# Lightning attention with a shrunk-tanh MLP: another order for the first group, tied sums, and a last product in three banks

## The chip, the cores and the metric

The kernel runs on one NeuronCore of a Trainium2 chip. The metric is the device time of one execution in microseconds (us), given as the median of several runs. A core has TensorE (PE, matrix products; the loads of its weights are listed apart as PEld), VectorE (DVE), ScalarE (ACT), GpSimd (POOL) and SyncE (SP, which here only issues DMAs). Each engine works off its own queue in order. Products land in PSUM[...].

## The reference, cut to what matters

Sizes: B = 4 sequences, H = 8 heads, S = 768 positions, D = 64; 3072 tokens, d_model 512, d_ff 2048. All in fp32, though w_in and w_out arrive as float64.

```python
# attention, in blocks; state kv_state per (b, h)
intra = einsum('bhic,bhjc->bhij', qb, kb) * Dmask
intra = einsum('bhij,bhjd->bhid', intra, vb)
inter = einsum('bhid,bhde->bhie', qb * lam_pow, kv_state)
out   = intra + inter
kv_state = lam_block * kv_state + einsum('bhsd,bhse->bhde', kb * rev_pow, vb)
# MLP on x, the attention output with tokens as rows
h = x @ w_in
g = h - tanh(h)
y = g @ w_out
```

## The kernel before

The sequence is cut into 6 groups `g` of 128 positions; a group holds a chunk of 128 positions of each of the 4 sequences `b`, so 512 tokens. The attention of a group goes in two halves of two chunks, `bs = (0, 1)` and `(2, 3)`. Four functions do a half:

- `att_transpose` (L251): q and k come in natural layout (`q_nat`, `k_nat`, `v_nat`, each 256 KB) and are transposed on PE against the identity (L264); ACT copies them to SBUF (L265). From the second group on, VectorE also scales q with the powers `fwd` (L269). From the third group on q and k are loaded otherwise, and this needs no PE.
- `att_scores` (L272): the products of k and q (L279, tile `sp`), and on VectorE the multiplication with the decay mask (L283, tile `ss`).
- `att_state` (L286): VectorE scales k in place (L294), PE forms k-transposed times v of both chunks (L299, tile `kv`), and the state takes it up. In the first group it is a plain copy out of PSUM (L306, on VectorE).
- `att_out` (L308): PE forms the state's part (L324, not in the first group) and the scores times v (L330, tile `op`), and ACT copies the result to `xt` (L334).

The tile pool keeps 2 buffers for q, 3 for k and 4 for v, so the fourth k of the first group waits until the first chunk's k has been read for the last time, in its state products. All loads of q, k, v and w_in are issued on SP's queue, in `load` (L126) and `load_weights` (L173); those of w_out and of the factors, and nearly all stores, on POOL's.

The weights come as 64-bit words. `weights(n)` (L183) brings the count of processed blocks to `n`: each block of 512 KB is loaded to `raw` (4 buffers) and rounded to fp32 by `round_block` (L217): two ACT operations (L227, L229) and four VectorE operations (L230, L232, L234, L236). w_in has 16 blocks, four for each quarter `u` of d_ff; w_out has 16, two for each `kt`.

The first group runs plain products: `up_plain(u, c)` (L467: products L473, tanh L476, subtraction L478) for 4 quarters `u` and 4 parts `c`, and `down_plain(kt)` (L482: products L490) for 8 steps `kt`. Between the steps the attention of the second group is done, and `sums_out` (L206) forms the combinations of w_out, which are stored as `factors` in DRAM. `powers` (L100) fills `fwd`, `sums_in(u)` (L198: L201 to L204) forms the combinations of w_in that the other five groups need. Those groups run a Strassen-Winograd form with seven products instead of eight: `up` (L389, products L397) and `down` (L431, products L439), in the order 1, 2, 6, 5, 7, 4, 3. In `down` products 1, 6, 7 and 4 accumulate one on another in one bank, `y`, and 5 and 3 in another, `z`; product 2 has the bank `w`. `evict` (L366) copies or adds the banks to the output tiles `o`: after product 7 the fourth output (L379, L380), after product 3 the part `12` (L386), stored by the lines under `finish` (L452; L460 for the last one, which goes in two halves).

The order of instructions on each engine is not simply that of the code. A scheduler sets it when the program is built: it goes by program order as priority, but where an instruction is not ready by its own model of times, a later one that is ready is taken first. `tc.keep_in_program_order(ins)` ties an instruction behind everything that was traced before it on its engine. Before the change only the transposes and k scalings of later groups (L259, L296) are tied. The main order around the change reads:

```python
p0, p1 = attention(0)      # pieces: transpose, scores, out, state for (0,1) and (2,3)
run(p0)
run(p1[0:1]); weights(1); run(p1[1:2]); weights(2); run(p1[2:4])
weights(KI); powers()
```

The `sums_in(u)` are traced after the last `down_plain` step.

Of the kernel before, what the change touches and what calls it, by code (L numbers as in the profile page):

```python
# [14 lines left out]
AL = mybir.AluOpType  # L15
# [8 lines left out]
def kernel(  # L24
# [75 lines left out]
    def powers():  # L100
        for j in range(2):
            nc.vector.tensor_copy(fwd[ts(j, 64), :, 0], lam_all.rearrange("s (p j) -> s j p", j=2)[ts(j, 64), j, :])
        m = 1
        while m < BLK:
            nc.vector.tensor_tensor(fwd[:, :, m:2 * m], fwd[:, :, 0:m], fwd[:, :, m - 1:m].to_broadcast([128, NP, m]),
                                    op=AL.mult)
            m *= 2
# [11 lines left out]
    def load_natural(g, b, names):  # L119
        for name, src, bufs in (("q", q, 2), ("k", k, 3), ("v", v, 4)):  # L120
            if name in names:
                x = io.tile([128, H, D], F32, name=f"{name}_nat", tag=name, bufs=bufs)
                nc.sync.dma_start(out=x, in_=src[b, :, ts(g, BLK), :].rearrange("h s d -> s h d"))
                raw[g, b][name] = x
# [73 lines left out]
    def sums_in(u):  # L198
        a11, a12, a21, a22 = (w1[u][:, 2 * c:2 * c + 2, r] for r, c in ((0, 0), (0, 1), (1, 0), (1, 1)))
        s1, s2, s4 = (ws[u][:, x] for x in range(3))  # L200
        nc.vector.tensor_tensor(s1, a21, a22, op=AL.add)  # L201
        nc.vector.tensor_tensor(s2, s1, a11, op=AL.subtract)
        nc.vector.tensor_tensor(a21, a11, a21, op=AL.subtract)
        nc.vector.tensor_tensor(s4, a12, s2, op=AL.subtract)  # L204

# [80 lines left out]
    def att_state(g, bs):  # L286
# [18 lines left out]
        else:  # L305
            nc.vector.tensor_copy(st, kv)  # L306

# [58 lines left out]
    def evict(key, n, dst, finish):  # L366

        y, z, w = (banks.get((key, x)) for x in "yzw")
        halves = [slice(None)] if key != ("down", NG - 1) else [slice(0, 256), slice(256, 512)]
        if n == 1:  # L370
# [6 lines left out]
        elif n == 7:  # L377
            for x in halves:
                nc.scalar.activation(dst(22)[:, x], y[:, x], AF.Copy)  # L379
            nc.vector.tensor_tensor(dst(22), dst(22), z, op=AL.add)  # L380
            finish(22, dst(22))
        elif n == 4:
            finish(21, y)
        elif n == 3:
            for x in halves:
                nc.vector.tensor_tensor(dst(12)[:, x], dst(12)[:, x], z[:, x], op=AL.add)  # L386
            finish(12, dst(12))
# [43 lines left out]
    def down(g, n):  # L431
        load_factor(stream.index((g, n)) + 2)
        wb = blks.pop((g, n))
        t, first = product_bank(("down", g), n)
        c = HIDAT[FACT[n][0]]
        for m in range(2):
            for kt in range(KH):
                a = hid[g, kt // 2, c].rearrange("q (m c) -> q m c", m=2)[:, kt % 2, ts(m, 128)]
                nc.tensor.matmul(out=t[:, m, :], lhsT=a, rhs=wb[:, kt, :], start=first and m == 0 and kt == 0,  # L439
                                 stop=kt == KH - 1, skip_group_check=True)  # L440
# [11 lines left out]
        def finish(c, src):  # L452
# [4 lines left out]
            o = dst(c).rearrange("q (m c) -> q m c", m=2)  # L457
            if g == NG - 1 and c == 12:
                for m in range(2):
                    nc.sync.dma_start(out=rows[:, m], in_=o[:, m])  # L460
            else:
                nc.gpsimd.dma_start(out=rows, in_=o)

# [37 lines left out]

    p0, p1 = attention(0)
    run(p0)
    run(p1[0:1])
    weights(1)
    run(p1[1:2])
    weights(2)
    run(p1[2:4])
    weights(KI)
    powers()  # L510
    for u in range(NU):
        for c in (11, 21, 12, 22):
            up_plain(u, c)
            weights(ready["done"] + 1)
    p0, p1 = attention(1)
    weights(len(blocks) - 2 * (KH - 2))
    more = [p0[0:1], p0[1:2], p0[2:], p1[0:1], p1[1:2], p1[2:]]
    for kt in range(KH):
# [4 lines left out]
        if kt < len(more):  # L523
            run(more[kt])
    for u in range(NU):
        sums_in(u)
    stage_open.__exit__(None, None, None)
# [53 lines left out]
```

## Time and profile before

| What | Value |
|---|---|
| Runs | 700.61, 700.79, 699.34 us; median 700.61 |
| Profiled execution | 699.61 us, of which the span is 697.8 |
| PE busy | 681.0 us, 98% of the span |
| VectorE, ACT, POOL busy | 353.0, 167.0, 55.9 us |
| PE's first operation | 5.10 us |
| First record of `up_plain`, first of `down_plain` | 31.44 us, 88.26 us |
| First product of the second group after `down_plain` | 161.5 us |
| End of the last product | 694.1 us |
| HBM read, written | 75.50 MB, 13.63 MB |

The span is what the profile shows between the first and the last event on the core; the 1.8 us beyond it lie around the program. Times of single instructions are from this one execution. In the lists, `L123` is a line of the kernel, `out<-in` the tiles, `xN` a count, and a bracket holds the idle time of the engine before the instruction and what ended it. `PEclk` or "granted clock" is the share of full speed that TensorE was given.

### The profile page before, as it was taken

Reading aid. Unit: us, or ns where it says so; the run is one execution under the profiler, and the core shown is the slowest. Engines: PE = TensorE matmul, PEld = TensorE weight load, DVE = VectorE, ACT = ScalarE, POOL = GpSimd, SP = SyncE. Lnnn points to the kernel's source line nnn. Section 1 sums busy time; section 2 is a strip of 40 time slices with the busy share of each in tenths; the row PEclk is TensorE's granted clock in tenths of the full one; section 3 lists DMA queues with packets and bytes.
Section 4 is the critical chain, followed back from the end, with each engine's and each line's share of the span. In section 5 each row is a group of like instructions: output and inputs, shape, how many; then the busy total and the mean of one; then the engine's idle time right before and its main releaser. Section 6 shows DMA issues by size and latency. Waiting matters only on the chain.

```text
span 697.8 us, 10361 instructions
## 1 busy us (share of the span) xinstructions
PE 681.0 (98%) x4096; PEld 571.2 (82%) x4096; DVE 353.0 (51%) x608; ACT 167.0 (24%) x281; POOL 55.9 (8%) x96
## 2 busy tenths in 40 slices
PE   6799999999999999999999999999999999999997
PEld 5688845557888888888888888888888888888886
DVE  4697988671566341456532346813346712254501
ACT  2554523323331010331000332001232101233100
POOL 0000312211000001000111000001000101000100
PEclk9899999999999999999999999999999999999999
DMA  9789957847225666263555702455700332400343
GB/s 167 175 209 241 257 163 232 248 123 212 34 32 129 167 172 178 34 117 92 131 179 138 188 0 70 118 160 157 177 1 1 121 136 80 147 1 0 113 145 105
DMA packets 143999, 89.82 MB, mean 129 GB/s; under 512 B 129808, under 2 KB 130064, under 8 KB 139472
## 3 DMA queue, kind: packets, MB, share of 16 engines
q0 software_dynamic: 11232, 58.46, 24.6%
q1 hardware_dynamic: 132576, 30.71, 23.2%
q8 instruction: 32, 0.52, 0.3%
q14 instruction: 15, 0.12, 0.1%
q10 hardware_dynamic: 144, 0.00, 0.0%
HBM read 75.50 MB, written 13.63 MB: 128 GB/s over the span
## 4 chain that ended last, share of the span: by engine, by line
PE 87%; DMA 5%; DVE 4%; ACT 1%; issue 1%; SPq 1%; ACTq 0%; DVEq 0%; POOLq 0%
PE y L439 20%; PE y L397 20%; PE z L439 10%; PE z L397 10%; PE op L490 7%; PE w L439 5%; PE w L397 5%; PE op L330 3%; PE sp L279 3%; DMA raw<-in_moe_w_in_dram 2%; DMA raw<-in_moe_w_out_dram 2%; PE op L324 1%; PE kv L299 1%; DVE g L478 1%; DMA k_nat<-in_k_dram 1%
## 5 line engine op out<-in xcount | busy, mean ns | idle before, releaser
L439 PE MATMUL y<-wb,g 128*128 128x256 f32 x640 | 142.3, 380 | 0.7 <-ACT o L379 0.7
L439 PEld LDWEIGHTS y<-wb,g 128*128 128x128 f32 x640 | 120.9, 190 | 18.1 <-ACT o L379 1.1
L397 PE MATMUL y<-xt,w 128*128 128x256 f32 x320 | 73.6, 380 | 0.0
L407 ACT ACTIVATE th<-g 128x512 f32<-128x512 f32 x60 | 37.8, 630 | 140.3 <-DVE g L373 86.1
L397 PEld LDWEIGHTS y<-xt,w 128*128 128x128 f32 x320 | 60.5, 190 | 8.9 <-issue 0.6
L490 PE MATMUL op<-wt,g 128*128 128x512 f32 x128 | 57.0, 597 | 1.7 <-DVE g L478 1.7
L408 DVE TENSOR_TENSOR g<-g,th 128x512 f32<-128x512 f32 x60 | 41.4, 689 | 32.5 <-ACT th L407 32.5
L426 POOL DMA_DIRECT2D wb<-factors x35 | 19.0, 544 | 477.5 <-PE y L439 366.8
L473 PE MATMUL h<-xt,w 128*128 128x256 f32 x256 | 56.7, 382 | 0.3 <-DVE w L236 0.2
L473 PEld LDWEIGHTS h<-xt,w 128*128 128x128 f32 x256 | 48.6, 191 | 8.1 <-DVE w L236 1.5
L283 DVE TENSOR_TENSOR ss<-sp,mask 128x512 f32<-128x512 f32 x48 | 30.9, 682 | 47.8 <-PE sp L279 47.8
L490 PEld LDWEIGHTS op<-wt,g 128*128 128x128 f32 x128 | 23.7, 190 | 30.0 <-issue 26.1
L380 DVE TENSOR_TENSOR g<-g,z 128x512 f32<-128x512 f32 x20 | 13.7, 685 | 49.9 <-ACT g L379 49.9
L397 PE MATMUL w<-xt,w 128*128 128x256 f32 x160 | 37.8, 379 | 0.0
L397 PE MATMUL y<-tt,w 128*128 128x256 f32 x160 | 37.8, 379 | 0.0
L397 PE MATMUL z<-tt,ws 128*128 128x256 f32 x160 | 37.8, 379 | 0.0
L397 PE MATMUL z<-xt,ws 128*128 128x256 f32 x160 | 37.8, 379 | 0.0
L397 PE MATMUL y<-tt,ws 128*128 128x256 f32 x160 | 37.8, 379 | 0.0
L439 PE MATMUL w<-wb,g 128*128 128x256 f32 x160 | 35.8, 382 | 0.0
L439 PE MATMUL z<-wb,gs 128*128 128x256 f32 x160 | 35.3, 379 | 0.0
L439 PE MATMUL z<-wb,g 128*128 128x256 f32 x160 | 35.3, 379 | 0.0
L397 PEld LDWEIGHTS y<-tt,w 128*128 128x128 f32 x160 | 30.4, 190 | 4.1
(88 smaller groups left out, 843.4 us busy)
## 6 DMA issues: line engine op xcount, KB each, us to landing
wb<-factors POOLq DMA_DIRECT2D x35, 1024.0 KB, 5.7
raw<-in_moe_w_out_dram POOLq DMA_DIRECT2D x16, 512.0 KB, 5.0
v_nat<-in_v_dram SPq DMA_DIRECT2D x24, 256.0 KB, 4.9
factors<-wt POOLq DMA_DIRECT2D x8, 768.0 KB, 4.7
k_nat<-in_k_dram SPq DMA_DIRECT2D x20, 256.0 KB, 4.8
out_dram<-o POOLq DMA_DIRECT2D x19, 256.0 KB, 5.3
raw<-in_moe_w_in_dram SPq DMA_DIRECT2D x8, 512.0 KB, 5.2
raw<-in_moe_w_in_dram SPq DMA_DIRECT2D x16, 256.0 KB, 5.2
```

The source lines that it names most:

```text
L279: nc.tensor.matmul(out=sp[j][:, p, :], lhsT=kt[ts(j, 64), p, :], rhs=qt[ts(j, 64), p, :], start=True, stop=True)
L283: nc.vector.tensor_tensor(ss[:, j], sp[j], mask[:, j], op=AL.mult)
L299: nc.tensor.matmul(out=kv[ts(j, 64), n, p, :], lhsT=kd[:, 2 * p + j, :], rhs=vn[:, 2 * p + j, :], start=n == 0 and p == 0, stop=True, skip ...
L330: nc.tensor.matmul(out=dst(n, p, j), lhsT=vn[:, 2 * p + j, :], rhs=ss[:, j, p, :], start=g == 0 and n == 0 and p % 2 == 0, stop=n == 1 and ...
L380: nc.vector.tensor_tensor(dst(22), dst(22), z, op=AL.add)
L397: nc.tensor.matmul(out=t[:, m, :], lhsT=wt[:, kt, ts(m, 128)], rhs=x[:, kt, :], start=first and m == 0 and kt == 0, stop=kt == 1, skip_gro ...
L407: nc.scalar.activation(th, src, AF.Tanh)
L408: nc.vector.tensor_tensor(dst(c), src, th, op=AL.subtract)
L426: nc.gpsimd.dma_start(out=blks[key], in_=factors[XAT[FACT[key[1]][1]]])
L439: nc.tensor.matmul(out=t[:, m, :], lhsT=a, rhs=wb[:, kt, :], start=first and m == 0 and kt == 0, stop=kt == KH - 1, skip_group_check=True)
L473: nc.tensor.matmul(out=hm[:, m, :], lhsT=w1[u][:, i, a, ts(m, 128)], rhs=xt[0, t][:, i, :], start=m == 0 and i == 0, stop=i == KI - 1, ski ...
L490: nc.tensor.matmul(out=obank[b], lhsT=g, rhs=wt[:, 2 * a:2 * a + 2, :], start=kt == 0 and a == 0, stop=kt == KH - 1 and a == 1)
```

## The change

The first group is written out chunk by chunk. For each half, each chunk is transposed and its scores formed before the next; before the scores of the second chunk of a half, `att_state` of the half is called. `weights(1)` stands after the transposes of the last chunk and `weights(2)` ahead of the last `att_out`. The state copy of the first group goes from VectorE to ACT. For the last chunk of the first group v is loaded ahead of k. The `powers` are called after the second quarter of `up_plain` and tied to program order. The `sums_in` are called in the last four steps of `down_plain`, one quarter a step, and tied as well. In the last group, product 3 of `down` no longer accumulates on product 5 in `z`: `z` is added to the output tile after product 7, and product 3 goes in three pieces to banks of their own: the first 128 rows with 256 columns, and the other 128 rows with 128 and 128 columns, each added to the output and stored from SP as it ends.

```diff
--- before.py
+++ after.py
@@ -99,11 +99,12 @@
 
     def powers():
         for j in range(2):
-            nc.vector.tensor_copy(fwd[ts(j, 64), :, 0], lam_all.rearrange("s (p j) -> s j p", j=2)[ts(j, 64), j, :])
+            tc.keep_in_program_order(nc.vector.tensor_copy(
+                fwd[ts(j, 64), :, 0], lam_all.rearrange("s (p j) -> s j p", j=2)[ts(j, 64), j, :]))
         m = 1
         while m < BLK:
-            nc.vector.tensor_tensor(fwd[:, :, m:2 * m], fwd[:, :, 0:m], fwd[:, :, m - 1:m].to_broadcast([128, NP, m]),
-                                    op=AL.mult)
+            tc.keep_in_program_order(nc.vector.tensor_tensor(
+                fwd[:, :, m:2 * m], fwd[:, :, 0:m], fwd[:, :, m - 1:m].to_broadcast([128, NP, m]), op=AL.mult))
             m *= 2
 
 
@@ -117,7 +118,8 @@
     at = {"loaded": 0}
 
     def load_natural(g, b, names):
-        for name, src, bufs in (("q", q, 2), ("k", k, 3), ("v", v, 4)):
+        for name, src, bufs in (("q", q, 2), ("v", v, 4), ("k", k, 3)) if (g, b) == (0, B - 1) else (
+                ("q", q, 2), ("k", k, 3), ("v", v, 4)):
             if name in names:
                 x = io.tile([128, H, D], F32, name=f"{name}_nat", tag=name, bufs=bufs)
                 nc.sync.dma_start(out=x, in_=src[b, :, ts(g, BLK), :].rearrange("h s d -> s h d"))
@@ -198,10 +200,9 @@
     def sums_in(u):
         a11, a12, a21, a22 = (w1[u][:, 2 * c:2 * c + 2, r] for r, c in ((0, 0), (0, 1), (1, 0), (1, 1)))
         s1, s2, s4 = (ws[u][:, x] for x in range(3))
-        nc.vector.tensor_tensor(s1, a21, a22, op=AL.add)
-        nc.vector.tensor_tensor(s2, s1, a11, op=AL.subtract)
-        nc.vector.tensor_tensor(a21, a11, a21, op=AL.subtract)
-        nc.vector.tensor_tensor(s4, a12, s2, op=AL.subtract)
+        for dst, x, y, op in ((s1, a21, a22, AL.add), (s2, s1, a11, AL.subtract), (a21, a11, a21, AL.subtract),
+                              (s4, a12, s2, AL.subtract)):
+            tc.keep_in_program_order(nc.vector.tensor_tensor(dst, x, y, op=op))
 
     def sums_out(kt):
         wt = pair[kt]
@@ -303,7 +304,7 @@
             nc.vector.tensor_tensor(st, st, lam_blk, op=AL.mult)
             nc.vector.tensor_tensor(st, st, kv, op=AL.add)
         else:
-            nc.vector.tensor_copy(st, kv)
+            nc.scalar.activation(st, kv, AF.Copy)
 
     def att_out(g, bs):
         half = bs[0] // 2
@@ -366,7 +367,8 @@
     def evict(key, n, dst, finish):
 
         y, z, w = (banks.get((key, x)) for x in "yzw")
-        halves = [slice(None)] if key != ("down", NG - 1) else [slice(0, 256), slice(256, 512)]
+        end = key == ("down", NG - 1)
+        halves = [slice(0, 256), slice(256, 512)] if end else [slice(None)]
         if n == 1:
             nc.scalar.activation(dst(11), y, AF.Copy)
         elif n == 2:
@@ -379,11 +381,12 @@
                 nc.scalar.activation(dst(22)[:, x], y[:, x], AF.Copy)
             nc.vector.tensor_tensor(dst(22), dst(22), z, op=AL.add)
             finish(22, dst(22))
+            if end:
+                nc.vector.tensor_tensor(dst(12), dst(12), z, op=AL.add)
         elif n == 4:
             finish(21, y)
         elif n == 3:
-            for x in halves:
-                nc.vector.tensor_tensor(dst(12)[:, x], dst(12)[:, x], z[:, x], op=AL.add)
+            nc.vector.tensor_tensor(dst(12), dst(12), z, op=AL.add)
             finish(12, dst(12))
 
     def up(g, u, n):
@@ -431,11 +434,26 @@
     def down(g, n):
         load_factor(stream.index((g, n)) + 2)
         wb = blks.pop((g, n))
+        c = HIDAT[FACT[n][0]]
+
+        def hidden(kt, m):
+            return hid[g, kt // 2, c].rearrange("q (m c) -> q m c", m=2)[:, kt % 2, ts(m, 128)]
+
+        if g == NG - 1 and n == 3:
+
+            rows = out.rearrange("(b s) d -> s b d", b=B)[ts(g, BLK), 0:2, 256:512]
+            for tag, bufs, m, c0, c1 in (("w", 1, 0, 0, 256), ("z", 1, 1, 0, 128), ("y", 2, 1, 128, 256)):
+                t = bank("end", tag, bufs)[:, 0:c1 - c0]
+                for kt in range(KH):
+                    nc.tensor.matmul(out=t, lhsT=hidden(kt, m), rhs=wb[:, kt, c0:c1], start=kt == 0, stop=kt == KH - 1)
+                o = hid[g, 12].rearrange("q (m c) -> q m c", m=2)[:, m, c0:c1]
+                nc.vector.tensor_tensor(o, o, t, op=AL.add)
+                nc.sync.dma_start(out=rows[:, m, c0:c1], in_=o)
+            return
         t, first = product_bank(("down", g), n)
-        c = HIDAT[FACT[n][0]]
         for m in range(2):
             for kt in range(KH):
-                a = hid[g, kt // 2, c].rearrange("q (m c) -> q m c", m=2)[:, kt % 2, ts(m, 128)]
+                a = hidden(kt, m)
                 nc.tensor.matmul(out=t[:, m, :], lhsT=a, rhs=wb[:, kt, :], start=first and m == 0 and kt == 0,
                                  stop=kt == KH - 1, skip_group_check=True)
         if n == 2:
@@ -455,11 +473,7 @@
                 nc.vector.tensor_copy(dst(c), src)
             rows = out.rearrange("(b s) d -> s b d", b=B)[ts(g, BLK), 2 * i:2 * i + 2, ts(j, 256)]
             o = dst(c).rearrange("q (m c) -> q m c", m=2)
-            if g == NG - 1 and c == 12:
-                for m in range(2):
-                    nc.sync.dma_start(out=rows[:, m], in_=o[:, m])
-            else:
-                nc.gpsimd.dma_start(out=rows, in_=o)
+            nc.gpsimd.dma_start(out=rows, in_=o)
 
         evict(("down", g), n, dst, finish)
 
@@ -499,19 +513,24 @@
         for fn, *args in pieces:
             fn(*args)
 
-    p0, p1 = attention(0)
-    run(p0)
-    run(p1[0:1])
-    weights(1)
-    run(p1[1:2])
-    weights(2)
-    run(p1[2:4])
+    for bs in ((0, 1), (2, 3)):
+        for b in bs:
+            att_transpose(0, (b,))
+            if b == 3:
+                weights(1)
+            if b % 2:
+                att_state(0, bs)
+            att_scores(0, (b,))
+        if bs[0]:
+            weights(2)
+        att_out(0, bs)
     weights(KI)
-    powers()
     for u in range(NU):
         for c in (11, 21, 12, 22):
             up_plain(u, c)
             weights(ready["done"] + 1)
+        if u == 1:
+            powers()
     p0, p1 = attention(1)
     weights(len(blocks) - 2 * (KH - 2))
     more = [p0[0:1], p0[1:2], p0[2:], p1[0:1], p1[1:2], p1[2:]]
@@ -522,8 +541,8 @@
             weights(ready["done"] + 2)
         if kt < len(more):
             run(more[kt])
-    for u in range(NU):
-        sums_in(u)
+        if kt >= KH - NU:
+            sums_in(kt - KH + NU)
     stage_open.__exit__(None, None, None)
     late["pool"] = ctx.enter_context(tc.tile_pool(name="late", bufs=8))
     up(1, 0, 1)
```

## Prediction

> **What bounds the kernel now.** I read the page first, for the engine that is full, then the chain of waits, then the timeline of the stretches where that engine is not full.
>
> ```profile
> span 697.8 us, 10361 instructions
> PE 681.0 (98%) x4096; PEld 571.2 (82%) x4096; DVE 353.0 (51%) x608; ACT 167.0 (24%) x281; POOL 55.9 (8%) x96
> PE   6799999999999999999999999999999999999997
> PE 87%; DMA 5%; DVE 4%; ACT 1%; issue 1%; SPq 1%; ACTq 0%; DVEq 0%; POOLq 0%
> ```
>
> TensorE is full from the third slice to the last but one. From 161.5 us to 679.3 us the chain is an unbroken row of products, and the change touches nothing there. So the whole gain or loss lies in three places: the start up to the first product of the first group (31.4 us), the change from up-projection to down-projection (88 to 97 us), and the tail after 694 us. PE's idle time is 697.8 - 681.0 = 16.8 us; about 5 of it is the first load, 4 the tail.
>
> The start, from the timeline (columns: start, length, engine, line, operation, tiles, count, idle before and its releaser):
>
> ```profile
> 11.90 1.14 SPq L123 DMA_DIRECT2D v_nat<-in_v_dram  x1
> ...
> 17.35 0.37 SPq L123 DMA_DIRECT2D k_nat<-in_k_dram  x1
> 17.77 1.87 SPq L168 DMA_DIRECT2D raw<-in_moe_w_in_dram  x2
> ...
> 23.80 0.66 ACT L227 ACTIVATE r<-raw 128x512 int32<-128x512 uint32 x1 [1.97 <-DMA raw<-in_moe_w_in_dram]
> ...
> 26.13 2.18 PE L330 MATMUL op<-ss,v_nat 128*64 128x128 f32 x17 [2.64 <-DVE ss L283]
> ...
> 31.55 0.69 DVE L306 COPY state<-kv 128x512 f32<-128x512 f32 x1 [1.44 <-PE kv L299]
> ```
>
> SP issues nothing between 13.0 and 17.35 us. The fourth chunk's k needs the buffer of the first chunk's k (three buffers), which is free only when the state products (L299) have read it, and those stand behind the scores and outputs of both chunks. All w_in loads queue behind that k. The DMA engines drain and then stand still, as the table of windows shows (after DVE, ACT and POOL come the granted clock, the DMA share and GB/s):
>
> ```profile
> 14.00:16.00 2.00, 2.00 (x28) 1.78 (x27) 1.52 (x3) 0.00 (x0) 0.00 (x0) 1.00 1.10 180
> 16.00:18.00 2.00, 2.00 (x51) 1.93 (x47) 0.17 (x1) 1.08 (x2) 0.00 (x0) 1.00 0.05 9
> 26.00:28.00 2.00, 1.87 (x18) 1.87 (x20) 2.00 (x5) 1.26 (x2) 0.00 (x0) 0.50 1.06 238
> 31.50:88.30 56.80, 56.48 (x258) 48.76 (x258) 50.83 (x103) 31.25 (x53) 6.58 (x11) 0.99 0.89 225
> ```
>
> The last row is the up-projection of the first group: PE is full, but VectorE has 50.83 us of work in 56.8, since it rounds the weights. In it the 256 products at 216 ns (6.91 us for 32 in the chain) take 55.3 us and end at 88.26 us, so their effective start is 88.26 - 55.3 = 33.0 us, though the first record is at 31.44: the first ones wait for rounded blocks (L236), the fourth of which is done at 37.5.
>
> The seam, from the timeline:
>
> ```profile
> 91.03 0.68 DVE L203 TENSOR_TENSOR w<-w 128x512 f32<-128x512 f32 x1
> 91.63 0.68 DVE L204 TENSOR_TENSOR ws<-w,ws 128x512 f32<-128x512 f32 x1
> 92.23 0.68 DVE L478 TENSOR_TENSOR g<-h,th 128x512 f32<-128x512 f32 x1
> ...
> 92.97 1.98 PE L490 MATMUL op<-wt,g 128*128 128x512 f32 x4 [1.11 <-DVE g L478]
> ...
> 95.49 1.98 PE L490 MATMUL op<-wt,g 128*128 128x512 f32 x4 [0.54 <-DVE g L478]
> ```
>
> The sums of w_in (L201 to L204), traced 50 us later, have been drawn ahead of the subtraction that the down-projection needs; PE waits 1.11 + 0.54 = 1.65 us. The tail:
>
> ```profile
> 694.12 0.75 DVE L386 TENSOR_TENSOR o<-o,z 128x256 f32<-128x256 f32 x2 [6.21 <-PE z L439]
> 694.61 0.84 SPq L460 DMA_DIRECT2D out_dram<-o  x2
> ```
>
> After the last product come two additions and two DMA issues in a row; the second issue starts at 695.1.
>
> **What the Trainium skill says.** "TensorE: Matmul & The Clock Gate", section "Architectural detail", has ScalarE and VectorE as strict FIFOs, and PE's matmuls in program order. The trace agrees: at 25.05 us VectorE holds a rounding that waited 2.09 us, and the ready mask multiplication (L283) that PE waits for comes behind it. The same page, "What's actually happening", says that the array falls to half rate after an idle window of some 3.4 us and recovers after a busy one. The trace agrees roughly: after the 2.64 us gap the granted clock is 0.50 from 26 to about 31.6 us. "DMA: Bandwidth & Descriptors", "Latency and other measured facts", speaks of some 2 us of fixed cost per DMA, mostly the receipt from memory; the last stores (128 KB) land 1.8 us after issue, so a smaller last store should save little by its size.
>
> **The change, part by part.**
>
> *State ahead of the second chunk's scores.* The first chunk's k transposes end at 7.35 us, ACT's copy at 7.98. Then, at the rates of the cold array seen here, come its scores (half of 3.72: 1.86 us, to 9.9), the second chunk's transposes (1.09 + 1.12 = 2.2, to 12.1) and the first chunk's state products (32 for two chunks take 1.09 us warm, so one chunk 0.55 warm and by estimate 1.1 cold, to 13.2). So k of the fourth chunk can be issued at about 13.3 instead of 17.35. The third chunk's loads are at most 0.5 us later, since the fourth q waits for the second chunk's q transposes (11.0 instead of 9.7) and SP has it at 10.6 now. Putting v ahead of k is worth nothing: SP already sends it first (11.90 against 17.35). What the DMA engines gain is the hole from about 15.8 to 18.7, that is 3 us, or up to 4.0 by SP's times; I take 3.5 for the stream of k and w_in. Everything SP holds behind k moves with it: the four first w_in blocks in six DMAs, then the next group's q, k, v. POOL's w_out loads move only as rounding frees their buffers.
>
> *What that is worth at the up-projection.* Lower end 3.0 us: the stream's shift, less 0.5 for the new order. Upper end: VectorE's queue also loses a 1.44 us wait and the copy behind it (L306, now on ACT), and eight sums that lie in 31.5 to 88.3 (eight at the 0.60 us pitch of the timeline: 4.8), and gains the powers (L102, L105: 0.35 + 1.85 = 2.2 us, formerly at 3.8 to 6.1 us): 3.5 + 1.4 + 4.8 - 2.2 = 7.5. PE takes that only as far as the attention of the second half, fed by the fourth k (landing 20.5 now, about 17 then), lets it start. I take **4.0 us**: the shift plus a little for the unblocked queue.
>
> *State copy on ACT.* Two copies of 128x512; the xt copies of the same shape take 594 ns, near the page "ScalarE: Activation LUTs" ("What ACT_TABLE_LOAD costs": 186 ns + 0.833 per element, 612 ns). ACT has 31.25 of 56.8 us of work, so 1.2 us is hidden; but ACT's roundings now stand behind a copy that waits for PE. Bounds: nothing, or the 1.44 us wait moved over. It is why I stay away from 7.5.
>
> *Powers and sums tied.* The powers leave VectorE's first 6 us, so the mask scans end 2.2 us earlier (the first k scaling, at 8.70, then waits only for PE); first used at 102 us, they have cover until then. The sums lose their place ahead of L478: **1.65 us** back at the seam (bounds 0.5, if other work fills the place, to 1.65). In 140 to 161.5 us VectorE has 12.2 us of work; 16 sums at 0.60 are 9.6, which with the sums of the next group's attention already in these 12.2 makes 21.8 against 21.5, with another 7.1 spare to 170. Only the first sums are needed early, and their turn is a step of 7 us each. I cost it at nothing; the cover is PE's 14 us of products of the last two steps.
>
> *Three banks at the end.* The 128-column products cost half of 216 ns, as the 128-column transposes do (0.44 us between groups of four): 16 x 0.216 + 32 x 0.108 = 6.91, as before; the double weight loads hide at that rate (nothing, by an estimate at most 0.5 us). The extra addition of z (0.69 us at 680.7) lies under the next product. After PE's end at 694.1 one addition of 128 columns (a 128x128 one of L105 takes 0.29) precedes the issue: 694.12 + 0.29 + 0.07 = 694.5 instead of 695.1: **0.6 us** (0.3 to 0.8). The wait of 0.75 us at 679.3 stays.
>
> Sum: 4.0 + 1.65 + 0.6 = 6.25 us. Against the profiled execution (699.61, span 697.8) that gives 693.4; it lies 1.0 below the median of the runs, 700.61. I forecast against the median: **694.4**.
>
> **The rivals.** *A, the forecast:* 694.4, with 690.0 for the upper ends (7.5 + 1.65 + 0.8 = 9.95, off 699.6 to 700.6) and 697 for the lower. *B, the up-projection stays bound by rounding:* the loads come earlier, but ACT's waiting copy or VectorE's order holds the fourth block; of the start only 1.0 remains. For it: VectorE's 89% in that stage; against it: the work that leaves its queue. 1.0 + 1.65 + 0.6 = 3.25, time 697.4. *C, slower:* in the second half, the scaling of the fourth k (L294) lands behind the first rounding on VectorE, since that rounding is traced ahead of it. State products and scores then wait on PE for the weights. If k and w_in are issued as late as now, the first block (23.8 us) needs 1.3 on ACT and 2.2 on VectorE, then come 0.7 scaling, 1.1 state, 1.0 scores, 1.4 masks, 1.0 outputs and 1.1 copies: 33.6 instead of 31.8, and some 2 us more with a cold array after a gap past 3.4 us. That is 4 us lost against 2.25 won: 702.4. It decides from the point where this k moves by less than 2 us; PE's short queue at the start speaks against it. *D, the change doesn't do what it says:* the scheduler already lays out the start as it likes, the loads stay where they are, and only seam and tail count: 2.25, time 698.4.
>
> **How the numbers follow.** Chances: A 0.62, B 0.20, C 0.10, D 0.08. About 0.2% (1.4 us) is what a measurement of this kernel can tell from no change. A, B and D lie beyond it on the fast side; I keep 0.06 for weak outcomes of B and D. So faster 0.84, same 0.06, slower 0.10. The range takes in A's bounds, B and D with the spread of the runs: 690.0 to 699.6.
>
> **What would show it.** Right: SP issues the fourth k near 13 us and the first w_in load near 14.5; no 2 us window under 100 GB/s between 14 and 30; the first raw block on ACT near 20; up-projection ends near 84; no wait of L490 on L478; sums between about 130 and 165 us; last store issued some 0.4 us after PE's end; the row of products from the second group on unchanged in length. Wrong: the fourth k still near 17 us; a gap of PE before 30 us longer than 3 us with clock 0.50 after it; L473 waiting for L236 more than the present 1.7 us; or products of the second group waiting for the sums.

## The result, and the profile after

The changed kernel takes 692.98 us in the median (692.67 to 693.28, 4 runs), against 700.7 us (699.34 to 701.08, 4 runs) for the one before: a ratio of 0.9893 with a 95% interval of 0.9876 to 0.991, or 7.7 us less. The forecast was 694.4, with a range of 690.0 to 699.6. The profiled executions lie a little closer together, 699.61 and 693.28; the stages below add up to their difference within 0.1 us.

The page of the changed kernel, the lines that answer to those shown of the kernel before (busy time by engine, PE's busy tenths, the chain by engine):

```profile
span 691.4 us, 10409 instructions
PE 678.4 (98%) x4112; PEld 569.2 (82%) x4112; DVE 353.2 (51%) x608; ACT 167.9 (24%) x283; POOL 55.8 (8%) x96
PE   6899999999999999999999999999999999999998
PE 94%; DMA 3%; DVE 2%; ACT 0%; issue 0%; SPq 0%; ACTq 0%; DVEq 0%
```

PE is as full as before, in a shorter span, and its share of the chain has risen from 87% to 94%: what went was time that the chain spent in DMAs, VectorE and ACT. PE's own busy time fell as well, from 681.0 to 678.4 us, though it does 16 products more. From the records of the products, the span splits like this (us; the second group's first product in the kernel before starts at 161.36, which the table further up gives as 161.5):

| Stage | before | after | gain |
|---|---|---|---|
| up to the first down-projection product of the first group | 88.26 | 84.84 | 3.42 |
| from there to the first product of the second group | 73.10 | 70.92 | 2.18 |
| from there to the end of the last product | 532.73 | 532.84 | -0.11 |
| from there to the end of the span | 3.70 | 2.80 | 0.90 |
| span | 697.8 | 691.4 | 6.4 |

The start, from the timeline of the changed kernel. Lines have moved: up-projection products are L487, their subtraction L492, down-projection products L504, the last step of a rounding L237, the sums L205:

```profile
13.16 1.09 SPq L125 DMA_DIRECT2D k_nat<-in_k_dram  x1
...
14.29 1.81 SPq L170 DMA_DIRECT2D raw<-in_moe_w_in_dram  x2
...
20.84 0.68 ACT L228 ACTIVATE r<-raw 128x512 int32<-128x512 uint32 x1 [1.75 <-DMA raw<-in_moe_w_in_dram]
...
27.18 0.70 PE L487 MATMUL h<-xt,w 128*128 128x256 f32 x2
...
44.59 40.41 PE L487 MATMUL h<-xt,w 128*128 128x256 f32 x186 [0.94 <-DVE w L237]
```

The fourth k is issued 4.2 us earlier, the first w_in load 3.5, and the first block reaches ACT 3.0 us earlier. In the table of windows (after the five engines come clock, DMA share, GB/s) the hole in the DMA traffic and the stretch at half clock that the prediction shows are both gone:

```profile
16.00:18.00 2.00, 2.00 (x24) 1.53 (x20) 0.23 (x1) 0.97 (x2) 0.00 (x0) 1.00 1.16 246
26.00:28.00 2.00, 1.51 (x16) 0.77 (x14) 2.00 (x5) 1.15 (x2) 0.00 (x0) 1.00 0.71 220
```

The whole first stage in the same table, first before, then after (PE's busy time and its count of products come first):

```profile
0.00:88.26 88.26, 77.58 (x480) 67.21 (x481) 66.89 (x140) 42.15 (x70) 7.27 (x17) 0.96 0.89 210
0.00:84.84 84.84, 75.42 (x480) 64.28 (x481) 63.00 (x132) 42.99 (x72) 7.90 (x18) 1.00 0.92 226
```

So of the 3.42 us that this stage gained, 2.16 us are shorter product time for the same 480 products, and 1.26 us are waits of PE that went.

The seam and the late sums, from the timeline:

```profile
84.84 7.03 PE L504 MATMUL op<-wt,g 128*128 128x512 f32 x16
...
155.42 0.68 DVE L205 TENSOR_TENSOR ws<-w,ws 128x512 f32<-128x512 f32 x1
155.76 1.89 PE L400 MATMUL y<-xt,w 128*128 128x256 f32 x8
```

The 16 products of the first step now run through in 7.03 us. The last of the sums starts at 155.42 us, when the second group begins, and no product waits for it. The tail:

```profile
681.41 7.19 PE L448 MATMUL end<-wb,g 128*128 128x256 f32 x48
688.63 0.29 DVE L450 TENSOR_TENSOR o<-o,end 128x128 f32<-128x128 f32 x1 [1.50 <-PE end L448]
688.95 0.33 SPq L451 DMA_DIRECT2D out_dram<-o  x1
```

The last store is issued 0.35 us after PE's end at 688.60, where it was 0.98 us (695.08 after 694.10).

### The profile page after: what moved, and what is told of

It reads as the page before. It is cut to its first block, busy times and chain, and to the rows that moved or that the text cites. A ratio compares the mean times of both kernels' runs of the same rounds, so it can differ in the third digit from the quotient of the medians.

```text
span 691.4 us, 10409 instructions
## 1 busy us (share of the span) xinstructions
PE 678.4 (98%) x4112; PEld 569.2 (82%) x4112; DVE 353.2 (51%) x608; ACT 167.9 (24%) x283; POOL 55.8 (8%) x96
## 4 chain that ended last, share of the span: by engine, by line
PE 94%; DMA 3%; DVE 2%; ACT 0%; issue 0%; SPq 0%; ACTq 0%; DVEq 0%
PE y L457 20%; PE y L400 20%; PE z L400 10%; PE z L457 9%; PE op L504 8%; PE h L487 6%; PE w L457 5%; PE w L400 5%; PE sp L280 3%; PE op L331 3%; DMA raw<-in_moe_w_in_dram 2%; PE op L325 1%; PE kv L300 1%; PE tp L265 1%; PE end L448 1%; DMA q_nat<-in_q_dram 1%
## 5 line engine op out<-in xcount | busy, mean ns | idle before, releaser
L487 PE MATMUL h<-xt,w 128*128 128x256 f32 x256 | 56.2, 381 | 0.9 <-DVE w L237 0.9
L504 PE MATMUL op<-wt,g 128*128 128x512 f32 x128 | 56.5, 595 | 0.0
L487 PEld LDWEIGHTS h<-xt,w 128*128 128x128 f32 x256 | 48.3, 190 | 8.3 <-DVE w L237 1.3
L504 PEld LDWEIGHTS op<-wt,g 128*128 128x128 f32 x128 | 23.8, 190 | 27.7 <-issue 27.0
L400 PEld LDWEIGHTS y<-tt,ws 128*128 128x128 f32 x160 | 30.4, 190 | 4.1
L400 PEld LDWEIGHTS z<-xt,ws 128*128 128x128 f32 x160 | 30.4, 190 | 4.1
```

The lines of the kernel that those rows point to most:

```text
L400: nc.tensor.matmul(out=t[:, m, :], lhsT=wt[:, kt, ts(m, 128)], rhs=x[:, kt, :], start=first and m == 0 and kt == 0, stop=kt == 1, skip_gro ...
L487: nc.tensor.matmul(out=hm[:, m, :], lhsT=w1[u][:, i, a, ts(m, 128)], rhs=xt[0, t][:, i, :], start=m == 0 and i == 0, stop=i == KI - 1, ski ...
L504: nc.tensor.matmul(out=obank[b], lhsT=g, rhs=wt[:, 2 * a:2 * a + 2, :], start=kt == 0 and a == 0, stop=kt == KH - 1 and a == 1)
```

## The experiments

Theory: the gain is made of three separate things, as the prediction has it: earlier loads through the freed k buffer, no sums ahead of the subtractions at the seam, a shorter tail. Rival: at the start it is VectorE's lighter queue (sums, powers and state copy moved) that counts, not the loads. The kernels were run in three sets, each on one chip beside the kernel before. Its median was 699.25, 699.59 and 699.41 us there, so ratios compare between sets better than times. The changed kernel itself was not in these sets: where a run is set against it, the ratios, the medians and the profiles are three readings, and they do not always agree. `start` is the first down-projection product and `seam` the time from there to the second group, both from the one profiled execution.

| Kernel | median, us | ratio to before (95%) | fourth k issued | start | seam | tail |
|---|---|---|---|---|---|---|
| before | 700.7 | | 17.35 | 88.26 | 73.10 | 3.70 |
| after | 692.98 | 0.9893 (0.9876 to 0.991) | 13.16 | 84.84 | 70.92 | 2.80 |
| after, old order | 694.92 | 0.9941 (0.9923 to 0.9958) | 16.79 | 86.24 | 70.91 | 2.8 |
| after, free sums | 694.43 | 0.9928 (0.9909 to 0.9946) | 13.15 | 84.64 | 73.19 | 2.8 |
| after, old tail | 693.3 | 0.9913 (0.9896 to 0.9931) | 13.16 | 84.66 | 70.92 | 3.7 |
| after, copy on VectorE | 692.94 | 0.9909 (0.9891 to 0.9927) | 13.17 | 84.05 | 70.92 | 2.8 |
| after, early powers | 691.65 | 0.9896 (0.9877 to 0.9916) | 13.14 | 83.52 | 70.91 | 2.8 |
| before, new order | 695.65 | 0.995 (0.9934 to 0.9967) | 13.02 | 85.07 | 72.09 | 3.7 |
| before, late powers | 698.75 | 0.999 (0.9979 to 1.0001) | 16.88 | 87.27 | 73.20 | 3.7 |
| before, spare k buffer | 694.02 | 0.9921 (0.9903 to 0.9938) | 11.87 | 84.52 | 71.07 | 3.7 |
| before, late tied sums | 696.46 | 0.9955 (0.9939 to 0.997) | 16.95 | 86.49 | 70.92 | 3.7 |
| after, bank for product 4 | 692.51 | 0.9891 (0.9872 to 0.9911) | 13.10 | 85.11 | 70.91 | 2.75 |
| the same with early powers | 691.19 | 0.9879 (0.9862 to 0.9896) | 13.09 | 84.68 | 70.92 | 2.8 |
| and with the copy on VectorE | 691.48 | 0.9882 (0.9866 to 0.9898) | 13.06 | 84.17 | 70.91 | 2.8 |

**The old order with all the rest.**

```diff
-    for bs in ((0, 1), (2, 3)):
-        for b in bs:
...
+    p0, p1 = attention(0)
+    run(p0)
+    run(p1[0:1])
...
```

> The changed kernel with only the order of the first group put back (transposes of both chunks, scores, outputs, state last), the tied sums and powers, the ACT copy and the three banks kept. Theory 1, the gain at the start comes from the earlier state products that free the first k buffer: the fourth k is issued near 17.3 us again, the first w_in near 17.8, the first down-projection product near 88 us instead of 84.8, and the run is some 3.4 us slower than the changed kernel (about 696.4). Rival, the gain at the start comes from VectorE's lighter queue (sums, powers and state copy gone): the loads go back to 17.4 us, but the down-projection still starts by 86 us and the run loses 1.2 us or less (about 694). Seam and tail stay at the changed kernel's: 71.1 us from the first down-projection product to the second group, 2.8 us after PE's end.

Its timeline:

```profile
16.79 0.37 SPq L125 DMA_DIRECT2D k_nat<-in_k_dram  x1
...
25.32 1.60 PE L331 MATMUL op<-ss,v_nat 128*64 128x128 f32 x18 [2.61 <-DVE ss L284]
...
86.24 7.03 PE L504 MATMUL op<-wt,g 128*128 128x512 f32 x16
```

The loads are late again, as theory 1 has it, and PE's wait of 2.61 us for the masks is back. But in the profile the start is only 1.4 us later than in the changed kernel: between the two expectations. By the ratios (0.9941 against 0.9893) the run loses some 3.4 us, as theory 1 has it, by the medians 1.9; how much the old order costs is known no better than that. The order is needed, and something else in the change counts at the start beside it: 2.0 us by the profiles (88.26 to 86.24). By the medians of its own set it is less: of 4.3 us in all, seam and tail (2.2 and 0.9 in the profiles) leave 1.2.

**The order alone, the powers alone, and the sums alone, on the kernel before.** The first takes the new loop over chunks into the kernel before:

```diff
...
+    for bs in ((0, 1), (2, 3)):
+        for b in bs:
+            att_transpose(0, (b,))
...
+            if b % 2:
+                att_state(0, bs)
+            att_scores(0, (b,))
...
```

> The kernel before with the new order of the first group alone (chunk by chunk, state ahead of the second chunk's scores); powers early and untied, state copy on VectorE, sums untied, old tail. Theory 1 (the state's place moves the loads, and that is most of the gain at the start): fourth k near 13.2 us, first w_in near 14.3, down-projection starting at 85.0 to 85.5 us instead of 88.3, wait at the seam (1.6 us) and old tail (3.7 us) as before: some 3 us faster than before. Theory 2 (order and powers each carry about half, as the run with the old order and all the rest, 86.2 us, suggests): loads as early, but the down-projection starts at 86 to 87 us: 1.4 to 2 us faster.

The start comes at 85.07, 3.2 us earlier, as theory 1 has it, and the run is 0.5% faster. So the order alone carries most of the start. This kernel loads k ahead of v as before, and its fourth k is issued at 13.02 us all the same: the exchange of v and k is not what brings it forward. The seam is 1.0 us shorter of itself, though the sums still stand there: at another state of the queues they cost less.

```diff
...
-    powers()
...
+        if u == 1:
+            powers()
```

> The kernel before with the powers alone moved behind the second quarter of the up-projection and tied. Theory 1: the powers in VectorE's first six microseconds delay nothing but the first scaling of k, which then waits for PE: fourth k at most 0.6 us earlier, down-projection at 87.5 us or later, under 0.8 us faster. Theory 2: they delay the mask and with it scores, state products and every load behind them: down-projection at 86.2 to 86.8 us, 1.5 to 2 us faster.

The fourth k is issued 0.5 us earlier and the start is 1.0 us earlier, but the ratio, 0.999 (0.9979 to 1.0001), can't be told from no change. The powers are not the missing 2 us.

```diff
...
-    for u in range(NU):
-        sums_in(u)
...
+        if kt >= KH - NU:
+            sums_in(kt - KH + NU)
```

> The kernel before with the sums of w_in alone called in the last four down-projection steps and tied. If the sums cost only the wait at the seam: that wait goes, the stretch from the first down-projection product to the second group falls from 73.3 to 71.1 us, the start of the down-projection stays within 0.5 us of 88.3 (or of 87.3, as the kernels with the old order scatter): 1.6 to 2.2 us faster. If they also delay the up-projection (the term that the prediction took as its upper end): down-projection 1 us or more earlier as well, 2.7 us or more faster.

The seam falls by 2.2 us exactly as expected, but the run gains 3.0 us in the medians, and the profile's start is at 86.49. By the numbers that is the second expectation: the sums also count at the start of the old order. A rival is the array's clock, which scatters there. The kernels with the late sums and with the late powers have nearly the same gap of PE, and both begin again at 25.78 us. The timeline, first with the late sums, then with the late powers:

```profile
25.78 1.37 PE L329 MATMUL op<-ss,v_nat 128*64 128x128 f32 x18 [2.69 <-DVE ss L282]
...
27.91 0.88 PE L329 MATMUL op<-ss,v_nat 128*64 128x128 f32 x12
...
28.95 1.35 PE L472 MATMUL h<-xt,w 128*128 128x256 f32 x5
```

```profile
25.78 1.37 PE L331 MATMUL op<-ss,v_nat 128*64 128x128 f32 x18 [2.80 <-DVE ss L284]
...
28.06 1.50 PE L331 MATMUL op<-ss,v_nat 128*64 128x128 f32 x12
...
29.92 0.80 PE L474 MATMUL h<-xt,w 128*128 128x256 f32 x1
```

The granted clock from 28 to 30 us, again late sums first:

```profile
28.00:30.00 2.00, 2.00 (x25) 1.83 (x26) 2.00 (x6) 1.79 (x4) 0.00 (x0) 1.00 0.66 160
```

```profile
28.00:30.00 2.00, 2.00 (x27) 1.88 (x23) 1.49 (x4) 1.51 (x3) 0.00 (x0) 0.50 0.71 168
```

After a gap of nearly the same length the array ran at full clock in the one execution and at half in the other, and the first up-projection product came 1.0 us later. In the profile of the kernel before the clock is 0.50 from 26 to 32 us; in all the profiles with the new order it is 1.00 there.

How much of it every run pays can be read from the runs, since the mean granted clock of each one is on record. (In the profile of the kernel before, the stretch between 24 and 34 us accounts for the whole of its 0.995: windows of 2 us at 0.84, three times 0.50, and 0.95.) Of the 41 executions of the kernel before in the three sets, 9 had a mean clock of 1.00 and took 698.5 us on average; the other 32, at 0.994 to 0.999, took 699.7 (the difference is 0.7 to 1.6 in the single sets). Of the kernels with the new order of the first group, 5 of 44 executions fell below 1.00, and none of the four of the changed kernel. So a lower clock goes with 1.2 us more, and most executions of the kernel before pay it: by this estimate some 0.9 us of the gain is the clock.

It does not explain the late sums. At 0.997 to 0.998 they took 696.9 us on average (4 runs) against 699.8 for the kernel before on the same chip below 1.00 (8 runs); at 0.999 and 1.00 they took 695.6 (2 runs) against 699.0 (3 runs). That is 2.8 and 3.4 us, and the seam is 2.2: by these few runs the sums cost the start of the old order another 0.6 to 1.2 us.

**The buffer alone.** The fourth k goes into a tile of the output pool, idle at that time; nothing else of the kernel before is changed.

```diff
-                x = io.tile([128, H, D], F32, name=f"{name}_nat", tag=name, bufs=bufs)
+                if (g, b, name) == (0, B - 1, "k"):
+                    x = opool.tile([128, H, D], F32, name="k_nat", tag="o")
+                else:
+                    x = io.tile([128, H, D], F32, name=f"{name}_nat", tag=name, bufs=bufs)
```

> The kernel before with one change: the fourth k of the first group goes into a buffer of the output pool, which is unused then, so that it waits for no other k; nothing else moves. If the early loads are the whole worth of the new order (the state's place matters only through the buffer): fourth k near 12 us, first w_in near 14, first block on ACT near 20.5, and a gain at the start as large as that of the new order alone (down-projection at the same time as there within 0.5 us). If the order also gains by itself, or the rounding's queue takes the gain back, the loads come early but the down-projection starts 1 us or more later than with the new order alone.

Its timeline:

```profile
11.87 1.14 SPq L126 DMA_DIRECT2D k_nat<-in_k_dram  x1
...
14.24 1.78 SPq L171 DMA_DIRECT2D raw<-in_moe_w_in_dram  x2
...
27.14 10.15 PE L476 MATMUL h<-xt,w 128*128 128x256 f32 x38 [2.34 <-DVE w L239]
...
84.52 7.18 PE L493 MATMUL op<-wt,g 128*128 128x512 f32 x16
```

This settles most of the start. With the old order, the old powers and the copy on VectorE, one buffer brings the loads as early as the new order does and the start to 84.52, within 0.6 us of the new order alone (85.07) and 0.3 us ahead of the changed kernel. The run is 0.79% faster, nearly three quarters of the whole gain, though 2.0 us of that is the seam. The state's place matters because it frees the buffer. PE even has a gap of 2.34 us here that the new order has not, and the clock after it is 0.50 from 28 to 30 us, as in the kernel before; the start is early all the same, since after the gap PE waits no more for rounding. So the worth of the early loads does not hang on the clock. What the buffer changes goes beyond the loads in one point: with them early, the scheduler puts three of the second half's mask multiplications on VectorE ahead of the first rounding, where the kernel before has one; that share was not measured apart. The seam is short here too, 71.07 us, though the sums are as free as before: on this queue the subtractions come in time.

**The sums untied again in the changed kernel.**

```diff
-        for dst, x, y, op in ((s1, a21, a22, AL.add), ...
-            tc.keep_in_program_order(nc.vector.tensor_tensor(dst, x, y, op=op))
+        nc.vector.tensor_tensor(s1, a21, a22, op=AL.add)
...
-        if kt >= KH - NU:
-            sums_in(kt - KH + NU)
+    for u in range(NU):
+        sums_in(u)
```

> The changed kernel with the sums of w_in again untied and traced after the last down-projection step. Theory 1: the scheduler draws them ahead of the subtractions again, L504 waits for L492 at the seam, the stretch from the first down-projection product to the second group is some 2.2 us longer (73.3 instead of 71.1), and the start of the down-projection comes 0 to 1 us later, since the sums are back in VectorE's queue of the up-projection: 2.2 to 3.2 us slower, about 695.6. Rival, the wait at the seam came from the older, later VectorE queue of the first group and not from the sums: no wait at the seam, under 0.7 us slower (about 693.4).

```profile
91.96 1.55 PE L505 MATMUL op<-wt,g 128*128 128x512 f32 x3 [1.62 <-DVE g L493]
```

The wait is back, this time at one place, and the seam is 2.27 us longer; the start is not later (84.64), so the sums cost nothing within the up-projection of the new order. The loss is 1.5 us by the medians, 2.1 by the profiles and 2.4 by the ratios. Tying the sums and tracing them in the last four steps were taken back together, so which of the two is needed is not shown.

**The old tail.**

```diff
-        if g == NG - 1 and n == 3:
...
-            return
...
+            for x in halves:
+                nc.vector.tensor_tensor(dst(12)[:, x], dst(12)[:, x], z[:, x], op=AL.add)
```

> The changed kernel with the last product as before: product 3 accumulates on product 5 in one bank, two additions of 256 columns, two stores. Theory 1: only the tail differs, 3.7 us from PE's end to the end of the span instead of 2.8: 0.9 us slower, about 693.9, the end of PE the same within 0.2 us. Rival, the 48 instructions of the split product cost PE something that the shorter tail must first pay back: PE's end comes 0.2 to 0.5 us earlier with the old tail, and the run is 0.4 to 0.7 us slower only.

The tail is 3.7 us again, 0.9 more, as theory 1 has it. Of the rival there is a trace: from the second group to PE's end the old tail takes 532.73 us and the new one 532.84, so the 16 more products cost 0.1. The run time, 693.3, can't be told from the changed kernel's; the stage is the evidence.

**The state copy and the powers in the changed kernel.**

```diff
-            nc.scalar.activation(st, kv, AF.Copy)
+            nc.vector.tensor_copy(st, kv)
```

> The changed kernel with the state copy of the first group on VectorE again. Theory 1, the copy was in the way only because of where it stood in the old order: with the state products early, its wait is short, the fourth rounded block and the first down-projection product move by 0.7 us (the copy's own length) or less, the run by less than 0.7 us. Rival, the copy's place on VectorE was a main part of the gain at the start: VectorE waits for PE for over 1 us between 20 and 30 us ahead of a rounding, the fourth block is done 1.5 us later or more, and the run loses 1.0 us or more (about 694).

The median is 692.94 us, with a start at 84.05: no loss. By the ratios (0.9909 against 0.9893) it would be 1.1 us slower, with intervals that overlap; the pair in one set below, 691.19 and 691.48 us, also finds the copy's place free within 0.3 us.

```diff
...
+    powers()
     for u in range(NU):
...
-        if u == 1:
-            powers()
```

> The changed kernel with the powers early and untied as before, so 2.2 us of VectorE work ahead of the masks. Theory 1: with the new order it costs nothing at the start, since the first k scaling would wait for PE until 7.37 us and the masks then end at 8.6: under 0.5 us either way, about 693. Theory 2: the masks hold up the first chunk's scaling and the state products, and the fourth k moves by up to 1.2 us: 0.7 to 2 us slower, 693.7 to 695.

The fourth k is no later (13.14), so theory 2 is out. Neither theory expected a gain. The median is 691.65 us, 1.3 below the changed kernel's, but the ratios are the same (0.9896 and 0.9893), so a gain is not shown. The profile has the start at 83.52, with no wait of the up-projection for a rounding, where the changed kernel has one of 0.94 us that ends at 44.59. That wait is not the price of the late powers: in the changed kernel VectorE does them only from 54.59 to 60.8 us, ten microseconds after it.

**A version past both.** One wait of 0.75 us, before product 4 of the last group, stands in both kernels. It goes if product 4 has a bank of its own and y is copied to that output beforehand; the first piece of product 3 then takes a buffer of y. A bank here is a PSUM tile of 128x512 fp32; the kernel keeps eight, four for the attention, two for `y`, and one each for `z` and `w`.

```diff
+            if end:
+                nc.scalar.activation(dst(21), y, AF.Copy)
...
+        own = g == NG - 1 and n == 4
+        if own:
+            banks[("down", g), "four"] = bank("end", "w", 1)
...
+            if end:
+                nc.vector.tensor_tensor(dst(21), dst(21), banks[key, "four"], op=AL.add)
```

> The changed kernel with, in the last group, product 4 in a bank of its own and y copied to its output tile before it, so that PE need not wait for ACT's copies at 673.7 us; the first piece of product 3 takes a buffer of y instead of w. If the 0.75 us wait is PE's own loss: it goes, with some 0.2 us of refilling, and the run is 0.75 to 1.0 us faster than the changed kernel (about 692.1). If the wait only moves to the banks of product 3 (which need the copies and the addition of z done): a gap of PE between 680 and 688 us, gain under 0.3 us.

> The changed kernel with early, untied powers and product 4 in a bank of its own. If the two gains add: 691.65 less 0.75 to 1.0, about 690.8, with the down-projection starting near 83.5 us and no wait of PE for rounded blocks in the up-projection. If the early powers' gain was chance: about 692.

> As the kernel with early powers and the bank of its own, with the state copy on VectorE besides. If the copy's place is free, as its own run on the changed kernel showed (692.94 against 692.98 us): the same as without it within 0.4 us. If what the early powers leave of VectorE's slack is used up by it: L487 waits for L237 again and it is 0.5 us or more slower.

The changed kernel, and then the one with the own bank, in the timeline:

```profile
674.40 7.17 PE L457 MATMUL y<-wb,g 128*128 128x256 f32 x32 [0.75 <-ACT o L381]
```

```profile
673.75 7.07 PE L468 MATMUL end<-wb,g 128*128 128x256 f32 x32
673.96 0.66 ACT L381 ACTIVATE o<-y 128x256 f32<-128x256 f32 x2 [13.22 <-PE y L468]
```

Product 4 now starts ahead of ACT's copies, and the stretch from the second group to PE's end falls from 532.84 to 531.83 us in all three kernels: 1.0 us, no new gap behind it. In the profiled span 0.8 of it arrives, since the start is 0.3 later (85.11 against 84.84); by the ratios, 0.9891 and 0.9893, it can't be told. With early powers as well the median is 691.19 us and the ratio 0.9879 (0.9862 to 0.9896), the best of the case; by the medians early powers give 1.3 us beside the kernel without them on the same chip (692.51), but single runs and intervals overlap, so this is a hint. Its profiled start, 84.68, is not the 83.52 of the early powers alone, so that start was at least in part chance; the median lies between the two expectations, 690.8 and 692. The copy on VectorE makes no difference there (691.48).

## Why the prediction was right, point by point

- **Early loads: right, and the main thing.** The fourth k was worked out for 13.3 us, the first w_in load for 14.5; they came at 13.16 and 14.29. The spare buffer shows that this is the cause. One of the signs named failed without harm: from 28 to 30 us the DMA engines moved 86 GB/s, under the 100 forecast.
- **Its worth, 4.0 us: the profiles give 3.42.** The shift arrived as 3.0 us at ACT's first block, so the lower end of the sum held. What the term lacked is the array's clock: it was read in the old trace but given no price. Of the 3.42 us, 2.16 are product time and only 1.26 waits, while the term counted a shift of the loads; that its size came close is in part luck. The prediction also took the half clock after the 2.64 us gap as agreeing with an idle window of some 3.4 us. It does not: gaps of 2.34 to 2.80 us, all shorter than that, were followed by half clock in four profiles, and one of 2.69 us was not.
- **The upper end, 7.5 us, was wrong in its working.** It counted eight sums (4.8 us) as a gain of the up-projection. With the new order, tying them left the start where it was (84.64 without, 84.84 with). With the old order, at like clock, the late sums gained 0.6 to 1.2 us beyond the seam, a fraction of the 4.8. The wait that left VectorE with the state copy was counted at 1.4 us as well; copying there again cost nothing that shows.
- **Powers late at no cost: not refuted.** Moving them to the up-projection was called covered, and after they run (54.59 to 60.8 us) PE waits for nothing more in the up-projection. Early powers had lower medians, 691.65 and 691.19 us against 692.98 and 692.51, but the ratios differ by 0.0003 the wrong way in the first pair and the runs overlap in the second. No mechanism for a gain was found.
- **The seam, 1.65 us: 2.18.** The mechanism was right. Mis-sized was the term for a gap, which counted the idle time alone. The 16 products of the first step took rows of 8, 4 and 4 (3.60, 1.98 and 1.98 us) with 1.65 us idle between them, 9.21 us in all, and 7.03 in one row after: the 2.18. The two gaps cost 0.53 beside their idle time, and the gap before product 4 likewise 0.26 beside its 0.75.
- **The late sums covered: right.** The last one starts at 155.42 us and no product waits, as worked out (21.8 us of work for 21.5).
- **The tail, 0.6 us: 0.90.** The issue came 0.63 us earlier, as worked out. Mis-sized was the store itself: the prediction took a fixed cost of some 2 us from the Trainium skill ("DMA: Bandwidth & Descriptors", section "Latency and other measured facts") and gave a smaller store nothing. But the two 64 KB stores landed 1.5 and 1.6 us after issue, where the 128 KB store ahead of them and both of the kernel before took 1.8, and the span ended 2.45 us after the last issue instead of 2.72.
- **Rivals.** B (the start held by rounding) happened in small. Counted as the prediction counts it, products and weight loads together, PE's wait for the last step of a rounding in the up-projection rose from 1.7 to 2.2 us (0.94 of it at 44.59), which it had named as a sign of being wrong; what brings that wait stays open. C did not come: the fourth k moved by 4.2 us, past the 2 us at which it would decide, and the clock stayed at 1.00. D did not come.

The stages of the profiles sum to 6.4 us, and the forecast was 6.25: errors of -0.6, +0.5 and +0.3 that cancel, by luck. The measured 7.7 us also holds the 1.1 us by which the profiled execution of the kernel before was faster than its median, and 0.3 by which that of the changed kernel was slower than its own.

## What to carry to other kernels

In an in-order DMA queue, look at the load that waits for a buffer and at everything behind it: here a 256 KB load held up 8 MB of weights, and one spare tile from a pool that was idle gave no less than the new order of the whole first group alone (0.79% and 0.5%). Work that is ready early but needed late can be drawn ahead of work on the path; tie it behind the work it must not pass, but into a stretch where its engine has slack. A gap of the matrix engine can cost more than its idle time: here 0.26 us for each restart, and after gaps of 2.3 to 2.8 us often a stretch at half clock. The mean granted clock of each run tells how often, without a profile of each.

## What the runs showed of the hardware

Gaps of PE of 2.34, 2.61, 2.64 and 2.80 us (spare k buffer, after with the old order, before, late powers) were followed by windows of 2 us with a granted clock of 0.50 to 0.58, and one of 2.69 us (late sums) by 1.00. It varies between executions of one kernel: six runs of the late sums had mean clocks from 0.997 to 1.00. At the start of an execution the listed clock can't be trusted: it is 1.00 in every window of 2 us up to 24 us in the kernel before, yet there the four transposes of a k took 1.12 us at 6.2 us and 0.60 at 18.2.

In the records, a wait cost the row of 128x512 products 0.26 us beside its idle time (0.53 for two gaps, whose ends the profile models), and the row of 128x256 products the same (1.01 us for a wait of 0.75). With the free sums one listed gap of 1.62 us went with 2.27, but there the row of 12 ahead of it was stretched as well (5.69 us).

Halving the last store to 64 KB brought its landing from 1.8 us after issue to 1.5 and 1.6, and the end of the span 0.27 us nearer to the last issue.
